# New ranks for a planned instruction order: one planner figure, own ranks for the last job

## The chip, the cores and the metric

The kernel runs on one core of a Trainium2 chip. A core has TensorE (PE) for matrix products, VectorE (DVE), ScalarE (ACT), GpSimd (POOL) and SyncE (SP), which here issues all transfers. Each engine works through its own queue in the order in which the program issued the instructions; they meet at semaphores. The metric is the device time of one execution in microseconds, lower is better. The page of the profile shows one profiled execution.

## The reference

The inputs are q, k and v of 4 batches, 8 heads, 768 positions and 64 elements. Attention keeps the first 4 positions (the sinks) and a window of 128:

```python
keep = is_sink | in_window          # pos < 4, or 0 <= row - column < 128
scores = np.where(keep, scale * q @ k.T, -1e9)
a = softmax(scores); attn = a @ v
```

The result, as 3072 tokens x of 512 elements, goes through a soft mixture of 8 experts with 4 slots each:

```python
logits = x @ phi                               # 3072 x 32
d = softmax over the tokens (logits)
slot_input = d.T @ x                           # 32 x 512
slot_out[e] = np.maximum(slot_input[e] @ w1[e], 0) @ w2[e]
c = softmax over the slots (logits)
out = c @ slot_out                             # 3072 x 512
```

Everything is float32. The expert weights are 32 MB; all of them are loaded once.

## The kernel before, in words

The attention is done in 12 jobs (line 690): for each of 4 batches three blocks of 256 positions with all 8 heads. A job n is made of steps:

- loads of k, q and v from HBM (`load`, line 712), into buffers that the next job uses again;
- `prep` (729): q and k are transposed by TensorE and copied out of PSUM to `qt` and `kt`;
- `softmax` (765), four tiles a job: scores on TensorE (rank S) into one of two `s` tiles of PSUM, masks and maxima on VectorE (M), exponentials on ScalarE (E), then the reciprocal of the sum on VectorE and the product with it on GpSimd (N), then copies of the sinks' weights on GpSimd (K0);
- `weights_transposed` (841, T), `sinks_transposed` (851, K) and `select` (863, sel), by which GpSimd cuts the window out of the transposed weights;
- `values` (875, val): the product with v, copied to `xt`, a single buffer;
- `natural` (906, xn): `xt` transposed to `xn`; and `moe.tokens` (307, tok): the logits of the job's tokens, their running maximum, exponentials, and the products that add up the slots' inputs.

A function `transpose` (699) makes each unit of transpositions: 16 small ones on TensorE for a pair of PSUM tiles, 8 in the first job's halves.

After the last job `moe.finish` (399, fin) closes the sums, and `moe.tail` (511) runs the two expert layers and the combination with c, with an order written out by hand. Before it, `stack` and `turn` (481, 494; tr) prepare c: a split into two parts on GpSimd and a transposition. The weights go through 24 slots of 1 MB; some of these hold attention data until the last jobs have read them.

The order of all steps up to the tail is set by a planner in the program itself (class `Plan`, line 141). Each step is added with a rank (`key`), its engine or a choice of two, and a figure for its time. `order` (167) fills the queues greedily. It keeps a time per engine; of the steps that could start at nearly the same earliest moment it takes the one with the lowest rank:

```python
_, t, i = min((steps[i][0], t, i) for t, i in at if t <= t0 + 0.02)
```

On TensorE the margin is 0.1, and a step with another mode of the array has 2.0 added to its rank and 0.15 (`SWITCH`) to its start. A rank in the table `CFG` (line 624) is an offset: job n uses `4.0 * n + x` (line 935), and tile `tl` of its softmax adds `tl`. The times are used only to make the order; the program has no clock, and on the chip each instruction waits for its operands. Matmuls of rank 900 and over are filler that keeps TensorE's clock up where it has nothing else to do.

Of the kernel before, what the change touches and what calls it, by code (L numbers as in the profile page):

```python
# [19 lines left out]
P = 128  # L20
# [120 lines left out]
class Plan:  # L141
# [19 lines left out]
    def add(self, key, eng, time, fn, r=(), w=(), new=None, last=None, mode=(128, 128)):  # L161

        self.steps.append((key, eng, time if isinstance(time, tuple) else (time,) * len(eng), fn,
                           tuple(r), tuple(w), () if new is None else new if isinstance(new, tuple) else (new,), last))
        self.modes.append(mode)
# [434 lines left out]
class Weights:  # L600
# [8 lines left out]
    def load(self, t):  # L609
# [3 lines left out]
        else:  # L613
# [7 lines left out]
NSLOT = 24  # L621
WARM = 8, 10, 64
PT = 3
CFG = {'prep': [12.61, 9.18],
       'load': [-3.38, -3.85],
       'v': [1.83, 0.85],
       'S': -10.57,
       'M': 2.63,
       'E': -12.68,
       'N': -12.34,  # L630
       'K0': 21.52,
       'T': [-16.0, -7.72],
       'K': -4.71,
       'sel': [-0.03, 28.43, 20.14, 29.01],
       'val': [24.82, -9.08, 25.23, 14.39],
       'xn': [-7.99],
       'tok': [6.92, -6.01, -11.1, -10.96, -2.5, 24.5, -4.05, 10.05, 14.87, -0.52, -10.02],
       'sm': 52.69,
       'sinks': 20.14,
       'tr': [105.63, 140.0, 48.77, 112.98, 90.29, 94.54, 115.57, 123.47, 139.69, 140.0, 40.36, 140.0, 113.15, 139.74, 77.9,  # L640
              132.05, 74.81, 133.34, 53.28, 101.21, 10.99, 140.0, 113.6, 29.98, 113.36, 90.1, 140.0],
       'w': [105.83, 8.0],
       'fin': [67.08, 31.69, -10.5, 14.26, -12.91, 95.11, 15.87, 23.84, 30.35, 16.96],
       'xn1': [13.16],
       'tok1': [-3.74, -12.85, -0.16, -12.31, 11.68, 14.4, -13.13, -12.37, -0.07, -12.63, 13.3]}


def window_path(ctx, tc, c, moe, q, k, v, phi, w1, w2, out):
# [50 lines left out]
    def transpose(key, srcs, r):  # L699

        hs = plan.psum(), plan.psum()

        def go(e):
            for a, src in enumerate(srcs()):
                for x in range(2):
                    i = slice(64 * x, 64 * x + 64)
                    nc.tensor.transpose(hs[x]["tile"][:, 64 * a:64 * a + 64], src[i], c.ident[i, i])

        add(key, "P", 0.45 if len(r) > 1 else 0.25, go, r=r, w=[h["name"] for h in hs], new=hs, mode=ROWS)
        return hs  # L710

    def load(key, n, kind, i):
# [128 lines left out]
    def weights_transposed(key, n, quad):  # L841
        gs = [4 * n + 2 * quad + odd for odd in range(2)]
        hs = transpose(key, lambda: [pts[g % PT][:, a, o:o + P] for g, o in zip(gs, (0, 4)) for a in range(4)],
                       [("pt", g % PT) for g in gs])
        for i in range(2):
            add(key, *COPY, lambda e, h=hs[i], i=i: copy(
                e, xws[quad][:, i, 0].rearrange("p h (o y) -> p o h y", o=2),
                h["tile"].rearrange("p (o h y) -> p o h y", o=2, h=4)),
                r=[hs[i]["name"]], w=[("xw", quad, i, 0)], last=hs[i])
# [83 lines left out]
    for n, (b, j) in enumerate(jobs):  # L933
        def t(x, n=n):
            return 4.0 * n + x

        for kind in range(2):
            for i in range(2):
                load(t(O["load"][kind]), n, kind, i)
            prep(t(O["prep"][kind]), n, kind)  # L940
        for i in range(2):
            load(t(O["v"][i]), n, 2, i)
        for tl in range(4):
            softmax({x: t(tl + O[x]) for x in ("S", "M", "E", "N", "K0")}, n, tl)
            if tl % 2:
                weights_transposed(t(O["T"][tl // 2]), n, tl // 2)
        if j == 0:
            add(t(O["sinks"]), "V", 0.9, lambda e, b=b: batch_sinks(nc, vsink, c, b), r=["v4s", "bm"], w=["vsink"])
        sinks_transposed(t(O["K"]), n)
        for quad in range(2):  # L950
            for i in range(2):
                select(t(O["sel"][2 * quad + i]), n, quad, i)
        for quad in range(2):
            values([t(x) for x in O["val"][2 * quad:2 * quad + 2]], n, quad)
        end = "1" if n == N - 1 else ""
        natural(t(O["xn" + end][0]), n)
        moe.tokens(plan, [t(x) for x in O["tok" + end]], b, j, half, xnb, (0, 1))
        if j == NJ - 1:
            if b == B - 1:
                moe.finish(plan, [t(x) for x in O["fin"]])  # L960

                for _ in range(WARM[2]):
                    h = plan.psum("s")
                    add(900.0, "P", 0.11, lambda e, h=h: nc.tensor.matmul(
                        h["tile"][:, 0, 0:64], lhsT=c.ident, rhs=c.ident[:, 0:64], start=True, stop=True),
                        r=[("sk", 0, 0)], new=h, last=h)
            last = ["sit"] if b == B - 1 else []
            moe.slot_softmax(plan, t(O["sm"]), b, [("lg", b, x, i) for x in range(NJ) for i in range(2)] + last)
# [237 lines left out]
```

## Time and profile before

| | us |
|---|---|
| median of 3 runs | 248.84 (248.19 to 251.78) |
| profiled execution | 248.67 |
| its span, first to last instruction | 247.0 |
| TensorE busy | 214.8 (87% of the span) |
| VectorE, ScalarE, GpSimd busy | 161.3, 151.1, 141.9 |
| HBM read, written | 52.53 MB, 6.29 MB |

Nearly all instructions are issued through a wrapper at line 127, so groups are told apart by the tiles that they write and read: `w` and `s` are PSUM tiles, `first` holds loaded q and k and later `xn` and `xt`, `wt` is any of the 1 MB slots (in the attention `kt`, the softmax's weights and v, later expert weights), `ident` is the identity of the transpositions. A row of a timeline gives the start in us from the span's start, the duration, engine, line, operation, tiles and count. A row of the busy time by stage gives the stage, its length, and for each engine the busy us and the number of instructions, then the clock granted to TensorE as a share of the full one, the share of the DMA engines and the GB/s. A row of waits gives who waited for whom: us in total, times, longest.

### The profile page before, as it was taken

Reading aid. Unit: us, or ns where it says so; the run is one execution under the profiler, and the core shown is the slowest. Engines: PE = TensorE matmul, PEld = TensorE weight load, DVE = VectorE, ACT = ScalarE, POOL = GpSimd, SP = SyncE. Lnnn points to the kernel's source line nnn. Section 1 sums busy time; section 2 is a strip of 40 time slices with the busy share of each in tenths; the row PEclk is TensorE's granted clock in tenths of the full one; section 3 lists DMA queues with packets and bytes.
Section 4 is the critical chain, followed back from the end, with each engine's and each line's share of the span. In section 5 each row is a group of like instructions: output and inputs, shape, how many; then the busy total and the mean of one; then the engine's idle time right before and its main releaser. Section 6 shows DMA issues by size and latency. Waiting matters only on the chain.

```text
span 247.0 us, 8602 instructions
## 1 busy us (share of the span) xinstructions
PE 214.8 (87%) x3356; PEld 152.0 (62%) x3356; DVE 161.3 (65%) x440; ACT 151.1 (61%) x577; POOL 141.9 (57%) x281
## 2 busy tenths in 40 slices
PE   7953899898999799999979899997999999999820
PEld 7733566576777567776747677664787534556520
DVE  4289568759899956889994888997544611225340
ACT  2167569869778886968888686888643411214320
POOL 2036687976857995885789497678995141000000
PEclk9996799999999999999999999999999999999985
DMA  5597989999899799999999999460149989999896
GB/s 117 114 199 157 169 255 280 257 268 287 240 213 285 239 284 262 281 251 205 265 202 245 242 335 198 91 215 1 31 160 330 372 333 344 348 349 367 315 319 204
DMA packets 102963, 59.44 MB, mean 241 GB/s; under 512 B 76292, under 2 KB 98820, under 8 KB 102916
## 3 DMA queue, kind: packets, MB, share of 16 engines
q1 hardware_dynamic: 102916, 58.83, 86.0%
q8 instruction: 28, 0.46, 0.8%
q14 instruction: 19, 0.16, 0.2%
HBM read 52.53 MB, written 6.29 MB: 238 GB/s over the span
## 4 chain that ended last, share of the span: by engine, by line
PE 51%; DVE 28%; ACT 13%; issue 4%; POOL 0%; ACTq 0%; DVEq 0%; POOLq 0%
PE w L127 34%; PE s L127 15%; DVE wt L127 13%; ACT wt L127 9%; DVE s L127 9%; DVE rs L127 2%; PE w L1158 2%; DVE first L127 1%; ACT wt L582 1%; ACT first L127 1%; DVE call L127 1%; DVE acc L127 1%; DVE sums L127 0%; DVE wt L567 0%; DVE vsink L127 0%
## 5 line engine op out<-in xcount | busy, mean ns | idle before, releaser
L127 ACT ACTIVATE wt<-s,wt 128x132 f32<-128x132 f32 x192 | 68.5, 376 | 10.7 <-DVE wt L127 4.5
L127 POOL TENSOR_TENSOR wt<-wt 128x528 f32<-128x528 f32 x96 | 63.8, 670 | 19.4 <-DVE wt L127 8.2
L127 POOL TENSOR_SCALAR_AFFINE_SELECT wt<-wt 128x512 f32<-128x512 f32 x88 | 54.4, 640 | 15.6 <-DVE sums L127 9.8
L127 PE MATMUL w<-wt 128*64 128x128 f32 (+3 forms) x550 | 50.7, 317 | 1.6 <-DVE wt L567 1.0
L127 PE MATMUL s<-wt,qt 64*64 64x196 f32 (+2 forms) x768 | 43.1, 332 | 10.0 <-ACT wt L127 7.0
L127 PEld LDWEIGHTS w<-wt 128*64 128x64 f32 (+2 forms) x550 | 35.9, 140 | 13.8 <-DVE wt L567 2.1
L127 ACT ACTIVATION_READ_ACCUMULATOR wt<-s,wt 128x1 f32 x192 | 40.5, 211 | 0.0
L127 PEld LDWEIGHTS s<-wt,qt 64*64 64x64 f32 x768 | 27.0, 136 | 20.1 <-ACT wt L127 10.5
L127 DVE TENSOR_REDUCE wt<-s 128x4 f32<-128x528 f32 x48 | 33.9, 707 | 1.7
L127 PE MATMUL w<-ident,wt 64*128 64x64 f32 (+1 forms) x442 | 28.9, 239 | 3.7 <-POOL wt L127 1.2
L127 ACT COPY wt<-w 128x512 f32<-128x512 f32 (+1 forms) x41 | 23.7, 581 | 11.7 <-PE w L127 8.6
L127 PEld LDWEIGHTS w<-ident,wt 64*128 64x128 f32 (+1 forms) x442 | 21.2, 142 | 13.2 <-issue 6.6
L127 DVE COPY wt<-w 128x512 f32<-128x512 f32 (+1 forms) x33 | 22.0, 666 | 10.8 <-PE w L127 10.8
L127 PEld LDWEIGHTS w<-ident,first 64*128 64x128 f32 x576 | 21.8, 141 | 10.7 <-issue 5.0
L127 PE MATMUL w<-ident,first 64*128 64x64 f32 x576 | 26.9, 231 | 1.5 <-ACT first L127 1.5
L127 ACT COPY first<-w 128x512 f32<-128x512 f32 x32 | 18.6, 592 | 15.5 <-PE w L127 15.4
L127 DVE COPY_PREDICATED s<-later,s 128x256 f32<-128x256 uint8 x48 | 20.4, 425 | 4.4 <-PE s L127 3.2
L127 DVE TENSOR_TENSOR wt<-wt 128x4 f32<-128x4 f32 x48 | 13.6, 283 | 10.2 <-ACT wt L127 9.0
L127 ACT ACTIVATE qt<-w 128x512 f32<-128x512 f32 (+1 forms) x25 | 14.4, 579 | 6.2 <-PE w L127 4.3
L127 PE MATMUL s<-wt 128*32 128x256 f32 x256 | 14.4, 380 | 0.0
L127 PE MATMUL w<-wt,si 128*32 128x512 f32 x112 | 14.1, 594 | 0.0
L127 POOL COPY wt<-wt 128x512 f32<-128x512 f32 (+2 forms) x13 | 5.7, 455 | 13.5 <-ACT wt L127 11.0
(115 smaller groups left out, 246.1 us busy)
## 6 DMA issues: line engine op xcount, KB each, us to landing
wt<-in_moe_w_dram SPq DMA_DIRECT2D x30, 1024.0 KB, 8.2
wt<-in_v_dram SPq DMA_DIRECT2D x24, 256.0 KB, 4.5
first<-in_q_dram SPq DMA_DIRECT2D x22, 256.0 KB, 5.5
first<-in_k_dram SPq DMA_DIRECT2D x22, 256.0 KB, 4.6
out_dram<-wt SPq DMA_DIRECT2D x4, 1024.0 KB, 7.6
first<-in_moe_w_dram SPq DMA_DIRECT2D x2, 1024.0 KB, 5.1
out_dram<-wt SPq DMA_DIRECT2D x3, 512.0 KB
first<-in_k_dram SPq DMA_DIRECT2D x4, 128.0 KB, 2.3
```

The costliest lines, as they stand in the source:

```text
L127: return self.tc.keep_in_program_order(f(*args, **kw))
L582: (nc.vector.tensor_copy if n % 2 else nc.scalar.copy)(ob[:, 2 * (n - n0):2 * (n - n0) + 2], yp)
L1158: nc.tensor.matmul(t[:, 0:P], lhsT=c.ident, rhs=c.ident, start=True, stop=True)
```

## The change

The planner's figure for a unit of transpositions goes from 0.45 to 0.5 us, for a unit of half the size from 0.25 to 0.27. The last job (n = 11) gets its own ranks for all steps of the softmax, the transposed weights, the selects and the values (`S1` to `val1`); it had its own before for `xn` and `tok` alone. All ranks in `CFG` have new values. No step is added or left out, and nothing else of the planner is changed.

```diff
-CFG = {'prep': [12.61, 9.18],
-       'load': [-3.38, -3.85],
-       'v': [1.83, 0.85],
-       'S': -10.57,
-       'M': 2.63,
-       'E': -12.68,
-       'N': -12.34,
-       'K0': 21.52,
-       'T': [-16.0, -7.72],
-       'K': -4.71,
-       'sel': [-0.03, 28.43, 20.14, 29.01],
-       'val': [24.82, -9.08, 25.23, 14.39],
-       'xn': [-7.99],
-       'tok': [6.92, -6.01, -11.1, -10.96, -2.5, 24.5, -4.05, 10.05, 14.87, -0.52, -10.02],
-       'sm': 52.69,
-       'sinks': 20.14,
-       'tr': [105.63, 140.0, 48.77, 112.98, 90.29, 94.54, 115.57, 123.47, 139.69, 140.0, 40.36, 140.0, 113.15, 139.74, 77.9,
-              132.05, 74.81, 133.34, 53.28, 101.21, 10.99, 140.0, 113.6, 29.98, 113.36, 90.1, 140.0],
-       'w': [105.83, 8.0],
-       'fin': [67.08, 31.69, -10.5, 14.26, -12.91, 95.11, 15.87, 23.84, 30.35, 16.96],
-       'xn1': [13.16],
-       'tok1': [-3.74, -12.85, -0.16, -12.31, 11.68, 14.4, -13.13, -12.37, -0.07, -12.63, 13.3]}
+CFG = {'prep': [14.14, 11.26],
+       'load': [-3.21, -5.66],
+       'v': [-1.5, -2.36],
+       'S': -2.69,
+       'M': -3.97,
+       'E': -13.55,
+       'N': -14.47,
+       'K0': 0.23,
+       'T': [-10.69, -13.82],
+       'K': 3.06,
+       'sel': [28.76, 0.08, 23.88, 3.39],
+       'val': [19.1, 22.33, 30.0, 14.34],
+       'xn': [4.68],
+       'tok': [29.91, 4.21, 24.58, 23.66, 30.0, 23.7, 18.05, 9.45, 30.0, 29.73, 12.4],
+       'sm': 28.75,
+       'sinks': 29.27,
+       'tr': [108.27, 115.31, 110.99, 111.87, 90.92, 75.69, 112.44, 97.39, 124.43, 88.85, 102.8, 105.1, 63.6, 137.13, 99.23,
+              103.23, 57.24, 128.11, 64.92, 73.8, 10.5, 69.95, 110.93, 42.9, 139.73, 94.35, 61.5],
+       'w': [90.76, 8.0],
+       'fin': [-0.34, -7.46, -22.01, 45.38, -18.68, 31.25, 57.82, 91.45, -23.97, -30.0],
+       'xn1': [12.91],
+       'tok1': [0.15, -10.01, 22.09, -11.24, -1.41, -9.06, -16.0, -1.4, -11.95, 1.64, -2.52],
+       'S1': -16.0,
+       'M1': 14.38,
+       'E1': 24.63,
+       'N1': -3.99,
+       'K01': -12.25,
+       'T1': [-12.94, -1.46],
+       'K1': 30.0,
+       'sel1': [9.32, -3.46, 0.09, -14.66],
+       'val1': [19.95, 14.0, -6.45, -11.32]}
...
-        add(key, "P", 0.45 if len(r) > 1 else 0.25, go, r=r, w=[h["name"] for h in hs], new=hs, mode=ROWS)
+        add(key, "P", 0.5 if len(r) > 1 else 0.27, go, r=r, w=[h["name"] for h in hs], new=hs, mode=ROWS)
...
+        end = "1" if n == N - 1 else ""
         for tl in range(4):
-            softmax({x: t(tl + O[x]) for x in ("S", "M", "E", "N", "K0")}, n, tl)
+            softmax({x: t(tl + O[x + end]) for x in ("S", "M", "E", "N", "K0")}, n, tl)
             if tl % 2:
-                weights_transposed(t(O["T"][tl // 2]), n, tl // 2)
+                weights_transposed(t(O["T" + end][tl // 2]), n, tl // 2)
...
-        sinks_transposed(t(O["K"]), n)
+        sinks_transposed(t(O["K" + end]), n)
         for quad in range(2):
             for i in range(2):
-                select(t(O["sel"][2 * quad + i]), n, quad, i)
+                select(t(O["sel" + end][2 * quad + i]), n, quad, i)
         for quad in range(2):
-            values([t(x) for x in O["val"][2 * quad:2 * quad + 2]], n, quad)
-        end = "1" if n == N - 1 else ""
+            values([t(x) for x in O["val" + end][2 * quad:2 * quad + 2]], n, quad)
```

## The prediction

> **What bounds the kernel now.** I read the page first, then the busy time of each engine by stage, then TensorE's waits in the middle of the run, then the timelines of the last job.
>
> ```profile
> span 247.0 us, 8602 instructions
> PE 214.8 (87%) x3356; PEld 152.0 (62%) x3356; DVE 161.3 (65%) x440; ACT 151.1 (61%) x577; POOL 141.9 (57%) x281
> PE 51%; DVE 28%; ACT 13%; issue 4%; POOL 0%; ACTq 0%; DVEq 0%; POOLq 0%
> ```
>
> ```profile
> core 0: us, PE busy (x) PEld busy (x) DVE busy (x) ACT busy (x) POOL busy (x), PEclk, DMA share, GB/s
> 0.00:45.16 45.16, 34.51 (x491) 26.08 (x494) 30.14 (x97) 26.23 (x107) 23.50 (x54) 0.92 0.80 183
> 45.16:87.19 42.03, 39.19 (x701) 28.56 (x701) 35.16 (x94) 33.72 (x136) 32.59 (x62) 1.00 0.95 260
> 87.19:129.34 42.15, 39.30 (x702) 28.70 (x702) 34.95 (x94) 33.94 (x136) 32.58 (x62) 1.00 1.05 249
> 129.34:171.50 42.16, 38.78 (x687) 28.45 (x687) 34.80 (x94) 33.52 (x134) 32.22 (x62) 1.00 0.74 196
> 171.50:195.45 23.95, 23.71 (x328) 18.53 (x327) 11.85 (x32) 12.38 (x43) 17.18 (x38) 1.00 0.57 196
> 195.45:247.00 51.55, 39.28 (x454) 21.71 (x454) 14.37 (x32) 11.33 (x27) 3.84 (x7) 0.93 0.96 325
> ```
>
> TensorE leads the chain of waits with 51%. The stages are cut where the trace repeats: from 45.16 on, one batch (three jobs) takes 42.03, 42.15 and 42.16 us. In each, TensorE is busy for 39.2 us of 42.1, VectorE 35, ScalarE 34, GpSimd 33. So the middle is bound by TensorE but for about 2.8 us a batch. The expert layers and the output begin at 195.45 and take 51.55 us.
>
> Which results TensorE waits for in the middle (45 to 180 us): us in total, times, longest.
>
> ```profile
> PE s L127 <- ACT wt L127: 5.1, 6, 1.2
> PE w L127 <- DVE lb L127: 2.0, 3, 0.9
> PE w L127 <- ACT first L127: 1.5, 3, 0.5
> ```
>
> These are 8.6 us: scores that wait until the exponentials have left a bank of PSUM (5.1), slot products that wait for the evicted weights `lb` (2.0), and transpositions to `xn` that wait for the eviction of the values (1.5). All that an order can win in the middle lies here; the 39 us a batch stay.
>
> **The change, part by part.** No instruction is added or removed; the same 8602 stand in another order on five queues. So every term is a wait that goes or comes.
>
> *The figure.* Sixteen transpositions are one unit:
>
> ```profile
> 88.02 0.71 PE L127 MATMUL w<-ident,first 64*128 64x64 f32 x16
> 88.66 0.50 PE L127 MATMUL w<-pst,vsink 128*128 128x256 f32 x2
> ```
>
> ```profile
> L127 PE MATMUL w<-ident,first 64*128 64x64 f32 x576 | 26.9, 231 | 1.5 <-ACT first L127 1.5
> L127 PE MATMUL w<-ident,wt 64*128 64x64 f32 x384 | 18.3, 231 | 1.9 <-POOL wt L127 1.2 <-ACT qt L127 0.7
> ```
>
> The next work starts 0.64 us after a unit's first (88.66 less 88.02). The planner's old figure with the switch of mode was 0.45 + 0.15 = 0.60, the new one gives 0.65. There are (576 + 384) / 16 = 60 units, so the old plan held TensorE free 60 x 0.05 = 3.0 us too early over the run. This doesn't shorten anything by itself. It also doesn't touch the figures of the copies out of PSUM, 0.51 on ScalarE and 0.61 on VectorE, which run longer:
>
> ```profile
> L127 ACT COPY wt<-w 128x512 f32<-128x512 f32 x39 | 23.0, 592 | 5.5 <-DVE wt L127 2.7 <-PE w L127 2.4
> L127 DVE COPY wt<-w 128x512 f32<-128x512 f32 x31 | 21.1, 682 | 6.8 <-PE w L127 6.8
> ```
>
> So the new plan is right about one engine and still some 0.07 to 0.08 us too early about each copy: not every wait it planned away will be away.
>
> *The middle.* `xn` goes from -7.99 to 4.68, over three jobs of 4 later in rank: the transpositions no longer jump in front as soon as the planner thinks the values are copied, and something else may stand between. I take their 1.5 us as gone. The maxima go from 2.63 to -3.97, so on VectorE they now precede the token maxima (-6.01 to 4.21), the `lb` copy (-4.05 to 18.05) and the sums (-0.52 to 29.73). That could shorten the 5.1 us on the exponentials; but at the first job of a batch VectorE masks as well as reduces, and these waits may be pure latency, so I count nothing. The `lb` copy falls in rank: its 2.0 us I leave as they are. Middle: -1.5 us, bounds -8.6 (all waits gone) and +5.4 (worked out under the slower rival).
>
> *The last job.* Its keys are now its own. In the trace it waits on GpSimd (rows of GpSimd, one of VectorE, then of TensorE):
>
> ```profile
> 176.99 0.29 POOL L127 CAST qt<-call 128x128 fp32r<-128x128 f32 x1
> 177.37 0.47 POOL L127 TENSOR_TENSOR qt<-call,qt 128x128 fp32r<-128x128 f32 x1
> 177.80 0.62 POOL L127 TENSOR_SCALAR_AFFINE_SELECT wt<-wt 128x512 f32<-128x512 f32 x1
> 178.40 1.06 POOL L127 TENSOR_TENSOR wt<-wt 128x528 f32<-128x528 f32 x1
> 179.42 0.62 POOL L127 TENSOR_SCALAR_AFFINE_SELECT wt<-wt 128x512 f32<-128x512 f32 x1
> 180.00 0.20 POOL L127 CAST wt<-wt 128x32 fp32r<-128x32 f32 x1
> ```
>
> ```profile
> 177.55 0.18 DVE L127 RECIPROCAL wt<-wt 128x4 f32<-128x4 f32 x1
> ```
>
> ```profile
> 181.35 1.32 PE L127 MATMUL s<-ident 128*128 128x64 f32 x10
> ...
> 182.54 0.48 PE L127 MATMUL w<-pst,vsink 128*128 128x256 f32 x2
> ```
>
> The last tile's reciprocal ends at 177.73, but its product on GpSimd starts at 178.40: a stack for the output (`qt<-call`) and a select went first, 0.67 us. Its sink copies start at 180.00, behind another select that was put between, 0.58 us. Meanwhile TensorE runs filler (`s<-ident`) from 181.35 until the sinks' weights are there at 182.54. In ranks (4 x 11 for the job, 3 for the tile): that stack had 53.28, the last tile's sink copies 47 + 21.52 = 68.52; now the stack has 64.92 and the copies 47 - 12.25 = 34.75, ahead of three of the four selects (53.32, 40.54, 44.09, 29.34). The product (47 - 3.99 = 43.01) is ahead of the stack too. I count 0.67 + 0.58 = 1.25, cut to 1.2, because the filler gives room for 182.54 - 181.35 = 1.19. Bounds: -4.1 if all filler went (34 matmuls at about 0.12 us, 1.19 / 10, from the rows above and the group below) and +1.5 if the two stacks pushed back (0.76 us each: 177.80 less 176.99, and as much again) end up in front of the expert layers.
>
> ```profile
> L127 PE MATMUL s<-ident 128*128 128x64 f32 x34 | 5.2, 278 | 0.0
> ```
>
> The chain behind the last values, up to 195.45, is serial with filler between; I leave it. The expert layers keep their 51.55 us as long as the weights come:
>
> ```profile
> 181.58 7.28 SPq L127 DMA_DIRECT2D wt<-in_moe_w_dram  x4
> 193.59 0.37 SPq L127 DMA_DIRECT2D first<-in_moe_w_dram  x1
> 197.40 20.81 SPq L127 DMA_DIRECT2D wt<-in_moe_w_dram  x9
> ```
>
> ```profile
> wt<-in_moe_w_dram SPq DMA_DIRECT2D x30, 1024.0 KB, 8.2
> ```
>
> ```profile
> 195.45:225.20 29.75, 29.06 (x322) 15.02 (x325) 9.24 (x24) 7.61 (x20) 3.84 (x7) 1.00 1.04 347
> ```
>
> Fourteen tiles (4 + 1 + 9) of 1024 KB, 1.05 MB, are issued from 181.58 on; at the 347 GB/s of the last row that is some 42 us, to about 224. The second half of that stage's products, behind 225.20, needs the last of them. I estimate that cover at 1 to 3 us. As the tiles' slots are freed by the last jobs, an earlier end moves both; if only the products moved, a gain beyond 3 us would be lost to DMA.
>
> *The start.* The first job's loads of v now come ahead of phi and the sink rows on SP; both are used many us later, and I count nothing. What matters here is TensorE's clock (last columns: clock, DMA, GB/s):
>
> ```profile
> 14.03:20.86 6.83, 3.38 (x60) 2.35 (x62) 5.65 (x22) 5.14 (x26) 3.34 (x6) 1.00 1.15 220
> 20.86:27.69 6.83, 4.78 (x56) 3.36 (x54) 4.61 (x11) 2.94 (x11) 5.46 (x11) 0.50 0.92 176
> 27.69:34.52 6.83, 5.80 (x103) 4.15 (x100) 5.13 (x13) 5.81 (x27) 4.59 (x8) 1.00 0.81 224
> ```
>
> After a stretch in which TensorE was busy for 3.38 of 6.83 us, the next 6.83 us ran at half clock; after one with 4.78 busy it was full again. If the new order fills the first stretch, up to 4.78 / 2 = 2.4 us are won; if another stretch is halved, up to 6.83 / 2 = 3.4 us are lost. I take nothing: few steps are ready then, and ranks decide only between ready ones.
>
> The Trainium skill ("TensorE: Matmul & The Clock Gate", Part 1) has the clock halved after an idle window of about 3.4 us. No gap of that length stands in this stretch, so the trace doesn't agree with that wording: here a busy half was enough. By the page alone, a second half-clock stretch (below, among the rivals) would need such a gap and have next to no chance; by the trace it keeps a small one.
>
> **The sum.** The profiled execution took 248.67 us, of which 247.0 are the span. 248.67 - 1.5 - 1.2 = 246.0; the median shown, 248.84, is 0.17 above the profiled one, so I say 246.1.
>
> **The rivals.**
>
> *Most waits go.* The search finds an order that fills two thirds of the 8.6 us (5.7) beside the last job's 1.2: 248.84 - 6.9 = 241.9. For it: VectorE, ScalarE and GpSimd each have 7 us or more free in a batch, and low-ranked token work can be slipped into TensorE's gaps. Against: the copies' figures are still short, and in the row of waits ScalarE, not TensorE's own length, was late.
>
> *The new figure does nothing on the chip.* The waits change place and sum to the same: 248.8. For it: TensorE had been later than planned, which hides the other engines' lateness; a plan packed tightly to a right figure shows it again.
>
> *Half clock a second time.* 248.84 + up to 3.4, say 251.5. It needs one more 6.83 us stretch near the start with half or less busy; the stretch from 27.69 has 5.80.
>
> *Slower: the token chain is starved.* Logits go from 6.92 to 29.91, behind the first values of the next job (4 + 19.1 = 23.1). The values can't be copied to `xt` until the logits have read the old ones. Where the values' product runs first, its PSUM bank stays held, and logits, `lb` and products then come due with nothing left to put between. Price: one wait as that for `lb`, 2.0 / 3 = 0.67 us, in each of 11 jobs, less the 2.0 that are there: +5.4, so 254.2. It decides from the point where, in most jobs, TensorE goes idle with the logits of the job before unfinished. Against it: the planner knows this dependence.
>
> **How the numbers follow.** Forecast 0.42, most waits go 0.20, nothing 0.22, half clock 0.06, starved tokens 0.10. The range 241.5 to 251.5 leaves out a quarter of the second, a third of the fourth and all of the fifth: 0.05 + 0.02 + 0.10 = 0.17. The forecast alone spans 244 to 248.5. Two per cent of 248.84 is 5.0 us, about what a measurement of this kernel can tell from no change: below 243.9 lie nine tenths of the second case and a tenth of the forecast, 0.18 + 0.04 = 0.22; above 253.8 six tenths of the last, 0.06; between, 0.72.
>
> **What would show it.** Right: the batches take 41.6 us (1.5 us over three), the wait for `first` is gone from TensorE's list, and the expert layers start near 192.7 with the same 51.5 us behind them. The last job's product on GpSimd would start as its reciprocal ends, and less filler would run before its values. Wrong: a batch over 42.1 us, waits of TensorE for `lb` or for evicted values in every job, a second stretch at half clock before 45 us, or expert layers longer than 52 us because weights come late. If the middle is unchanged and the start differs by 2 us or more, the term that I set to nothing was the one that counted.

## The result and the profile after

The changed kernel takes 257.31 us (median; 254.67 to 257.51) where the kernel before, beside it, took 249.18. The ratio is 1.031, with a 95% interval of 1.026 to 1.036: slower. The forecast of 246.1 missed, and so did its range of 241.5 to 251.5. The profiled execution took 257.51 us, 255.7 of them the span.

From the page of the kernel after: the span, the busy times, and TensorE's clock in 40 slices.

```profile
span 255.7 us, 8637 instructions
PE 224.6 (88%) x3362; PEld 156.8 (61%) x3362; DVE 166.9 (65%) x437; ACT 152.3 (60%) x580; POOL 143.0 (56%) x281
PEclk9967599999998999998899999889999999999995
```

TensorE has six records of matmuls more (all filler; a matmul that isn't a transposition leaves two records in these traces) and yet is busy 9.8 us longer (224.6 to 214.8). The clock row says where to look: a dip over three slices at the start (6, 7, 5) and an 8, or two, at three places in the middle. The same row of the kernel before has a dip over two slices at the start and none in the middle:

```profile
PEclk9996799999999999999999999999999999999985
```

The busy times of the kernel after by stage (columns as in the prediction: stretch and length, busy time and count of each engine, clock, DMA share, GB/s). The cuts are laid so that each stage holds TensorE's instructions of before to within ten.

```profile
0.00:46.74 46.74, 36.91 (x483) 28.68 (x485) 32.57 (x97) 26.17 (x107) 23.56 (x54) 0.85 0.75 172
46.74:91.06 44.32, 41.58 (x707) 29.27 (x707) 36.40 (x92) 33.22 (x133) 32.80 (x62) 0.96 0.88 249
91.06:135.38 44.32, 41.56 (x705) 29.55 (x702) 36.56 (x94) 34.41 (x138) 32.83 (x62) 0.96 0.95 249
135.38:179.75 44.37, 40.95 (x689) 28.95 (x685) 36.34 (x94) 34.29 (x137) 32.83 (x62) 0.96 0.71 179
179.75:204.27 24.52, 24.33 (x338) 19.38 (x335) 10.80 (x33) 12.83 (x44) 17.10 (x38) 1.00 0.54 194
204.27:255.70 51.43, 39.27 (x455) 21.00 (x454) 14.23 (x32) 11.34 (x27) 3.85 (x7) 0.94 0.96 324
```

Against the rows of before, the start is 1.6 us longer (46.74 to 45.16), the three batches 2.3, 2.2 and 2.2, the last job 0.6 (24.52 to 23.95), the expert layers 0.1 shorter. These add up to the 8.7 us by which the span grew. In a batch the idle time is the same (44.32 - 41.56 = 2.76 after, 42.15 - 39.30 = 2.85 before); the busy time grew, at a mean clock of 0.96 where 1.00 stood.

The stretches of the kernel after, up to the expert layers, in which the granted clock is 0.50:

```profile
14.30:21.13 6.83, 5.64 (x71) 4.61 (x73) 5.86 (x15) 3.43 (x16) 3.76 (x8) 0.50 0.86 167
24.55:31.37 6.82, 6.10 (x66) 4.42 (x66) 4.29 (x12) 2.41 (x10) 3.36 (x8) 0.50 0.41 67
75.75:79.16 3.41, 3.41 (x22) 1.92 (x16) 1.81 (x5) 2.12 (x13) 2.22 (x5) 0.50 1.00 405
120.12:123.53 3.41, 3.41 (x22) 1.94 (x16) 1.79 (x5) 2.06 (x12) 2.17 (x5) 0.50 0.88 242
164.49:167.91 3.42, 3.42 (x22) 1.94 (x16) 1.77 (x5) 2.04 (x12) 2.15 (x6) 0.50 0.02 5
sum 23.89, PE 21.97 PEld 14.82 DVE 15.52 ACT 12.06 POOL 13.66; mean PE 4.39 PEld 2.96 DVE 3.10 ACT 2.41 POOL 2.73
```

TensorE works 21.97 us at half clock; before it was the 4.78 us of the one stretch that the prediction shows. At full clock that work takes half the time, so the growth costs (21.97 - 4.78) / 2 = 8.6 us. That is the size of the whole loss, in the two profiled executions.

A second account of the same, over one stretch from 8 us to the start of the expert layers (before, then after):

```profile
8.00:195.45 187.45, 169.03 (x2871) 123.97 (x2871) 144.42 (x387) 138.31 (x548) 136.80 (x263) 0.98 0.85 222
```

```profile
8.00:204.27 196.27, 178.88 (x2878) 129.38 (x2878) 150.18 (x384) 139.44 (x551) 137.86 (x263) 0.94 0.80 212
```

Idle is the length less the busy time: 18.4 before, 17.4 after, so the new order has 1.0 us *less* idle time. Taking half of the half-clock work off the busy time leaves 166.6 and 167.9 us of work: 1.3 more, of which some 0.7 is the six records of filler (0.12 us each). The rest of the difference is the clock. Both accounts rest on one profiled execution of each kernel.

**Why the clock fell in the middle.** TensorE in the windows of equal length that end where the three half-clock stretches begin:

```profile
72.33:75.75 3.42, 1.86 (x23) 1.18 (x26) 3.29 (x11) 3.28 (x13) 3.34 (x8) 1.00 1.06 259
116.70:120.12 3.42, 1.85 (x24) 1.18 (x26) 3.26 (x12) 3.33 (x13) 3.34 (x7) 1.00 1.06 211
161.08:164.49 3.41, 1.84 (x27) 1.18 (x26) 3.25 (x11) 3.36 (x13) 3.33 (x7) 1.00 0.37 84
```

It is busy for 54% in each. The stretches at half clock begin whole multiples of 3.41 us apart: from 75.75 to 120.12, and from there to 164.49, it is 44.37 us, 13 times 3.413. So the clock is set in windows that lie on one grid through the trace. The least busy window on the grid of the kernel before, in its middle, had 2.18 of 3.41 us, 64%, and the clock stayed at 1.00 behind it:

```profile
164.22:167.63 3.41, 2.18 (x60) 1.53 (x56) 3.34 (x10) 3.18 (x19) 2.72 (x6) 1.00 0.48 131
```

Laid at any place, not only on the grid, the least busy 3.41 us of the three batches of before hold 2.30, 2.31 and 2.05 us of work (from 82.68, 124.82 and 166.40). So the idle time of a batch hasn't grown; the new order has gathered it at one place, the third job. There is one thing more. A batch with its stretch takes 44.32 to 44.37 us, 13 windows, so the gap falls on the same place of a window in each batch, while the 42.15 us of a batch of before are 12.35 windows. That the stretches repeat for this reason is worked out from the lengths, not tested. TensorE's timeline in the third job of the first batch, with the idle time before a group and what ended it in brackets, and the waits of the whole middle (46 to 180 us):

```profile
72.93 0.71 PE L127 MATMUL w<-ident,wt 64*128 64x64 f32 x15 [0.49 <-ACT lt L127]
73.87 0.33 PE L127 MATMUL w<-ident,lt 128*128 128x128 f32 x1 [0.23 <-ACT qt L127]
74.34 0.52 PE L127 MATMUL w<-ident,wt 128*128 128x128 f32 x2
75.56 0.96 PE L127 MATMUL w<-first,lb 128*32 128x256 f32 x8 [0.69 <-DVE call L127]
```

```profile
PE s L127 <- ACT wt L127: 3.6, 9, 1.2
PE w L127 <- DVE call L127: 2.1, 3, 0.7
PE w L127 <- ACT lt L127: 1.5, 3, 0.5
PE w L127 <- DVE pst L127: 1.0, 1, 1.0
PE w L127 <- ACT qt L127: 0.7, 3, 0.2
```

The waits for `lb` (2.0) and nearly all of those for `first` (1.5) are gone, as are 1.5 us of those for the exponentials; the waits for `call`, `lt`, `pst` and `qt` came. The sum was 8.6 us and is 8.9.

What made `lt` late stands on VectorE, ScalarE and GpSimd (rows of each, in that order; the step `sums<-sums` is the minimum that merges the new token maximum, which is kept negated, with the old one):

```profile
70.64 0.80 DVE L127 TENSOR_TENSOR vsink<-wt,bm 128x512 fp32r<-128x512 f32 x1
71.37 1.02 DVE L127 TENSOR_TENSOR sums<-sums 128x1 f32<-128x1 f32 x1
...
75.19 0.22 DVE L127 COPY call<-w 128x64 f32<-128x64 f32 x1
```

```profile
72.42 0.36 ACT L127 ACTIVATE lt<-w,sums 64x128 f32<-64x128 f32 x1 [1.00 <-DVE sums L127]
```

```profile
70.87 1.50 POOL L127 TENSOR_TENSOR wt<-wt 128x528 f32<-128x528 f32 x1
```

A minimum of 128 single values took 1.02 us; one of the same steps in the kernel before takes 0.16 (at 110.99). It began beside a large product on GpSimd and ended (72.39) as that ended (72.37). The exponentials of the token weights on ScalarE needed that minimum and waited 1.00 us for it, and TensorE waited 0.49 us for them. Behind the minimum VectorE then works off four steps of the maxima (72.59 to 74.7) before it copies `call`, and the PSUM bank that the slot products need is held until that copy is done. The copy's rank (the last of `tok`) went from -10.02 to 12.4 and that of the maxima (`M`) from 2.63 to -3.97, so the two changed places.

### The profile page after: what moved, and what is told of

It is laid out like the page before. It is cut to its first block, busy times and chain, and to the rows that moved or that the text cites. A ratio compares the mean times of both kernels' runs of the same rounds, so it can differ in the third digit from the quotient of the medians.

```text
span 255.7 us, 8637 instructions
## 1 busy us (share of the span) xinstructions
PE 224.6 (88%) x3362; PEld 156.8 (61%) x3362; DVE 166.9 (65%) x437; ACT 152.3 (60%) x580; POOL 143.0 (56%) x281
## 4 chain that ended last, share of the span: by engine, by line
PE 55%; DVE 22%; ACT 16%; issue 3%; POOL 0%; ACTq 0%; DVEq 0%; POOLq 0%
PE w L127 40%; PE s L127 14%; ACT wt L127 12%; DVE wt L127 9%; DVE s L127 6%; DVE sums L127 3%; DVE first L127 2%; PE w L1167 1%; ACT wt L582 1%; ACT first L127 1%; ACT lt L127 1%; DVE vsink L127 1%; ACT sums L127 0%; DVE wt L567 0%; DVE phi L127 0%
## 5 line engine op out<-in xcount | busy, mean ns | idle before, releaser
L127 POOL TENSOR_TENSOR wt<-wt 128x528 f32<-128x528 f32 (+1 forms) x96 | 64.4, 674 | 29.3 <-DVE wt L127 22.1
L127 PE MATMUL w<-wt 128*64 128x128 f32 (+3 forms) x550 | 53.6, 330 | 1.9 <-DVE wt L567 1.0
L127 PE MATMUL s<-wt,qt 64*64 64x196 f32 (+2 forms) x768 | 45.0, 340 | 10.2 <-ACT wt L127 3.9
L127 PEld LDWEIGHTS w<-wt 128*64 128x64 f32 (+2 forms) x550 | 37.7, 147 | 15.5 <-issue 2.5
L127 ACT ACTIVATION_READ_ACCUMULATOR wt<-s,wt 128x1 f32 x192 | 41.9, 218 | 0.0
L127 ACT COPY wt<-w 128x512 f32<-128x512 f32 (+1 forms) x45 | 25.5, 581 | 13.6 <-PE w L127 10.9
L127 PE MATMUL w<-ident,wt 64*128 64x64 f32 (+1 forms) x442 | 30.5, 245 | 2.3 <-ACT lt L127 1.5
L127 DVE COPY wt<-w 128x512 f32<-128x512 f32 (+1 forms) x29 | 18.9, 655 | 11.4 <-ACT wt L127 7.6
L127 DVE COPY first<-w 128x512 f32<-128x512 f32 x25 | 17.0, 679 | 8.0 <-PE w L127 7.8
L127 ACT COPY first<-w 128x512 f32<-128x512 f32 x23 | 13.7, 594 | 8.6 <-PE w L127 8.0
```

Of the source, the lines that this page charges most:

```text
L127: return self.tc.keep_in_program_order(f(*args, **kw))
```

## The experiments

**The two parts apart.** First the figure alone, with the ranks of before:

```diff
-CFG = {'prep': [14.14, 11.26], ...
+CFG = {'prep': [12.61, 9.18], ...     (all ranks of before, for the last job too)
```

> The old ranks with the new figure (0.5 and 0.27) alone. Theory: the new order loses its time by where the new ranks put VectorE's and GpSimd's work at the third job of each batch, and TensorE then runs one stretch of 3.4 us a batch at half clock; the figure alone doesn't do that: 246 to 251 us, no half-clock stretch between 35 and 195 us. Rival: any order made with the new figure leaves TensorE idle more often: 253 us or more.

Measured: 254.65 us (252.94 to 260.31), 1.022 [1.015, 1.029]. The figure alone, on the ranks that stood beside the old one, costs 1.5 to 2.9%. My theory, a figure that does no harm, fell, and the profiled execution (260.31 us) has three stretches at half clock in the middle (from 47.77, 78.50 and 109.22) where I had expected none. But two of the four runs had a mean clock of 0.966, about that of the kernel before beside them (0.965 to 0.967 in four of its eight runs), and still took 252.94 and 253.28 us. So what these two runs lose, 4 to 5 us, can hardly be half clock. No profiled execution shows what it is.

Then the ranks alone, with the old figure:

```diff
-        add(key, "P", 0.5 if len(r) > 1 else 0.27, go, ...
+        add(key, "P", 0.45 if len(r) > 1 else 0.25, go, ...
```

> The new ranks with the old figure (0.45 and 0.25). Theory: the ranks carry the loss: 253 to 258 us. Rival: the ranks are sound and only fit a plan with their own figure; with the other figure the order is reshuffled and the time is anywhere, then the collision of the third job isn't a matter of ranks: 247 to 251 us would speak for that.

Measured: 258.84 us (255.69 to 260.48), 1.033 [1.027, 1.038]. Its interval overlaps that of the change as a whole. Each part loses alone, and together they lose about what the ranks lose. The new ranks are no better with the new figure than with the old one, as far as these runs can tell.

**The last job's own ranks.**

```diff
-            softmax({x: t(tl + O[x + end]) for x in ("S", "M", "E", "N", "K0")}, n, tl)
+            softmax({x: t(tl + O[x]) for x in ("S", "M", "E", "N", "K0")}, n, tl)
                 (the same for "T", "K", "sel" and "val")
```

> The new kernel, but the last job takes the ranks that all other jobs have (softmax, transposed weights, selects, values). My prediction had the last job's own ranks worth 1.2 us: then 258.5 us. Rival: the stretch from the last job's values to the expert layers is as long with either: 257.3 within 0.5 us. If the own ranks do harm: below 256.5 us.

Measured: 259.65 us (259.2 to 260.08), 1.045 [1.044, 1.047]. The own ranks are worth some 2 us, but not where I had put them: from the sink product of the last job to the expert layers this kernel takes 24.40 us, the change 24.52. By the account from 8 us on it has 21.5 us of idle time against 17.4: TensorE's waits for `call` are 3.6 instead of 2.1 us over the three batches, and one wait near 21 us for VectorE is 2.3 us instead of 0.5. How ranks of the last job come to change the order ahead of it was not followed further.

**The minimum out of GpSimd's way.** Here the token maximum stays in PSUM, in a free column of the logits' tile, so that the minimum reads one operand from PSUM and one from SBUF. The order is that of the change to the last step.

```diff
+        first = (lambda: L["tile"][:, P:P + 1]) if n else (lambda: new)
 ...
-            new, L["tile"][:, 0:P], op=ALU.max, axis=AX.X, negate=True), ...
+            first(), L["tile"][:, 0:P], op=ALU.max, axis=AX.X, negate=True), ...
 ...
-            plan.add(key, "V", 0.07, lambda e: nc.vector.tensor_tensor(new, new, old, op=ALU.min),
+            plan.add(key, "V", 0.07, lambda e: nc.vector.tensor_tensor(new, first(), old, op=ALU.min),
```

> The new kernel in its exact order; the token maximum is left in PSUM, so that the step that merges it with the old one (VectorE, 128x1) reads one operand from SBUF instead of two. Theory: in the new kernel this step takes 1.02 us beside a product of GpSimd at the third job of each batch, against 0.15 elsewhere, because the two engines exclude each other there; the exponential, lb and TensorE's products come late by that, and the idle time brings half clock. Then the step falls to about 0.2 us, the three half-clock stretches of the middle (75.7, 120.1, 164.5) go, a batch takes about 42 instead of 44.3 us, and the time is 250 to 252.5 us. Rival: the order alone (maxima ahead of lb) leaves TensorE idle: the step is shorter, the half-clock stretches stay, 256 to 257.5 us.

Measured: 255.01 us (254.58 to 257.07), 1.029 [1.023, 1.034]; the interval overlaps that of the change (1.026 to 1.036), so a gain isn't shown, and the time lies between the theory's range and the rival's. VectorE's timeline at the place that was shown above:

```profile
69.64 0.80 DVE L127 TENSOR_TENSOR vsink<-wt,bm 128x512 fp32r<-128x512 f32 x1
70.45 0.16 DVE L127 TENSOR_TENSOR sums<-w,sums 128x1 f32<-128x1 f32 x1
70.53 0.85 DVE L127 TENSOR_TENSOR wt<-wt 128x4 f32<-128x4 f32 x1
```

The minimum takes 0.16 instead of 1.02 us, and now the next small step with two operands in SBUF takes 0.85: the collision moved on by one step. The mean of all 11 minima says the same (before, after, this kernel; busy us, mean ns):

```profile
L127 DVE TENSOR_TENSOR sums<-sums 128x1 f32<-128x1 f32 x11 | 2.2, 201 | 0.2
```

```profile
L127 DVE TENSOR_TENSOR sums<-sums 128x1 f32<-128x1 f32 x11 | 5.9, 535 | 0.3
```

```profile
L127 DVE TENSOR_TENSOR sums<-w,sums 128x1 f32<-128x1 f32 x11 | 1.7, 158 | 0.6 <-ACT lt L127 0.3
```

So the price of that step comes from GpSimd's work beside it, and hangs on where its operands lie. The Trainium skill ("SBUF — State Buffer", section "Who interferes with whom") has a VectorE instruction with two SBUF inputs contend with a GpSimd instruction that reads SBUF; the trace agrees: 1.02 us with both in SBUF, 0.16 with one of them in PSUM, in the same order.

Of the three half-clock stretches of the middle the one near 75 us is gone; those near 118.0 and 162.4 stayed. That isn't the collision's doing. First the least busy 3.41 us at any place in the first and the second batch, then the windows on the grid that hold most of them:

```profile
71.07:74.48 3.41, 1.79 (x23) 1.02 (x20) 3.28 (x10) 3.36 (x14) 3.33 (x7) 1.00 0.91 229
113.71:117.12 3.41, 1.79 (x23) 1.02 (x20) 3.28 (x10) 3.36 (x14) 3.33 (x7) 1.00 1.13 225
```

```profile
70.23:73.64 3.41, 2.32 (x35) 1.50 (x35) 3.29 (x8) 3.14 (x13) 3.33 (x6) 1.00 0.72 163
114.60:118.02 3.42, 1.88 (x13) 0.90 (x13) 3.29 (x9) 3.42 (x18) 3.25 (x8) 1.00 1.05 205
```

The gap is the same in both batches, and as wide as in the change (1.79 us of work, there 1.84 to 1.86). But the grid, counted back from the stretch at 118.02 by 14 windows to 70.23, cut it otherwise in the first batch: the window held 2.32 us, and the clock stayed at 1.00. So this run doesn't show that the collision gathers the idle time. It shows something better: what one stretch costs in the same kernel and the same execution. From the third job of one batch to the third job of the next, without a stretch and with one:

```profile
75.06:117.69 42.63, 39.79 (x705) 28.61 (x701) 36.23 (x93) 34.34 (x138) 32.63 (x62) 1.00 0.95 249
117.69:162.06 44.37, 41.75 (x706) 29.51 (x702) 36.15 (x94) 34.04 (x136) 32.72 (x62) 0.96 0.90 240
```

The same work takes 1.74 us longer, about half of the 3.41 us at half clock; the idle time is 2.84 and 2.62 us. And a batch of the new order at full clock is still 0.5 us longer than one of before (42.63 against 42.15 us), with the same idle time (2.85) and TensorE busy for 39.79 instead of 39.30 us.

**Filler in the gap.** Small products on the identity, in the third job of each batch only: two ahead of the transposition of `lt`, six ahead of the slot products.

```diff
+            if n % 3 == 2:
+                for _ in range(6):
+                    nc.tensor.matmul(S["tile"][:, 0:64], lhsT=c.ident, rhs=c.ident[:, 0:64], start=True, stop=True)
                 (ahead of the slot products; two such into T["tile"] ahead of the transposition of lt)
```

> The new kernel in its exact order, with filler added on TensorE at the third job of each batch only: 2 small products (128x64) into the empty PSUM tile before the transposition of lt and 6 into the empty tile before the slot products, where TensorE stood idle 0.2 and 0.7 us. Nobody waits for them. Theory (half clock is what costs): TensorE is busy for about 80% instead of 54% of the stretch before, the three half-clock stretches of the middle go, each worth half of 3.41 us = 1.7: 257.3 - 5.1 = 252.2 us, range 251 to 253.5. Rival (the half clock only falls into time in which TensorE has slack, the other engines set the pace): the stretches go, but the time stays within 1.5 us of 257.3; or they stay, because filler of that kind doesn't count: 257 to 259.

Measured: 258.08 us (257.31 to 266.23), 1.033 [1.024, 1.041], no gain, as the rival had it. The same with the minimum in PSUM as well:

> The filler of the run before this one and the token maximum left in PSUM, together. Theory: the collision of VectorE and GpSimd and the half clock are two costs: the collision is worth some 0.7 us by itself (2.4 us measured, less one half-clock stretch of 1.7 that went with it), so about 251.5 us. Rival: it acted only by way of the half clock: as with the filler alone, within 0.5 us.

Measured: 264.82 us (260.63 to 266.69); the runs spread too far for an interval, and neither expectation came true. TensorE at the place, in the kernel with both:

```profile
74.71 1.52 PE L127 MATMUL w<-ident 128*128 128x64 f32 x12 [0.63 <-DVE call L127]
```

The filler writes to the tile of the slot products, so it waited for the same bank that they wait for. It stood behind the gap, not in it, and added 1.5 us a batch. So neither run is the test that it was meant to be. Two readings are still of use. With the filler alone four of five runs had a mean clock of 0.964 or 0.965, where the change had 0.938 to 0.948, and yet took 257.3 to 258.2 us: the clock rose, by some 5.6 us over the span, and the time did not fall. The filler, at 1.5 us in each of four jobs, would eat about that, but no profiled execution shows one of these runs. In the second of the two kernels the window ahead of a half-clock stretch that begins at 118.52:

```profile
115.10:118.52 3.42, 2.31 (x35) 1.46 (x27) 3.29 (x9) 3.37 (x14) 3.34 (x7) 1.00 1.05 234
```

Here 2.31 of 3.42 us busy, 68%, was followed by half clock, where 64% in the kernel before was not. The busy share alone doesn't decide. In this window stood, behind the end of a unit of scores, transpositions and products with 64 columns. The Trainium skill ("TensorE: Matmul & The Clock Gate", Part 4) says that transpositions don't count as busy in the same way; that fits this window, but no run here tried transpositions against products at the same share.

**A dense product in the gap.** Placed where nothing holds it up: behind the transpositions of the sinks of the jobs 3, 6 and 9, into the free half of their own PSUM tile, one product of 128x128 by 128x256 with a weight tile, which is loaded anyway, as its data.

```diff
+            if n and n % 3 == 0:
+                nc.tensor.matmul(h["tile"][:, 256:512], lhsT=c.ident, rhs=wts[0][:, 0:256], start=True, stop=True)
```

> The new kernel in its exact order, with one dense product (128x128 by 128x256, a loaded weight tile as data) added behind the sinks' transpositions of jobs 3, 6 and 9, in the empty half of their PSUM tile. That place is the idle 0.7 us ahead of the slot products; the tile is free there, which the tile of the filler before was not. Theory: half clock is the loss. TensorE's work at half clock falls from 21.8 us by the 3 x 3.4 us of the middle, half of which is time: 257.3 - 5.1 = 252.2, range 251 to 254. If only some stretches go, 1.7 us for each that goes. Rival (half clock only fills time that TensorE would wait anyway): the stretches go and the time stays above 256.

Measured: 254.43 us (253.0 to 257.1), 1.019 [1.015, 1.024], against 1.031 [1.026, 1.036] for the change; just above the theory's range. TensorE at the place in the second batch, and the two windows of the grid on which the gap falls there:

```profile
120.49 0.60 PE L127 MATMUL w<-wt,ident 128*128 128x256 f32 x2
121.36 0.64 PE L127 MATMUL w<-first,lb 128*32 128x256 f32 x8 [0.27 <-DVE call L127]
```

```profile
116.24:119.65 3.41, 2.58 (x52) 1.80 (x48) 3.34 (x9) 2.36 (x12) 3.41 (x4) 1.00 0.78 173
119.65:123.07 3.42, 3.00 (x25) 1.69 (x27) 3.29 (x9) 3.42 (x17) 2.75 (x8) 1.00 1.03 226
```

In the second and third batch the wait for `call` shrank to 0.27 and 0.26, and the clock stayed at 1.00. The least busy 3.41 us at any place of the second batch now hold 2.28 us (117.94 to 121.35), where the change has 1.85 in a window. So the product narrows the gap, but here the grid cuts it in two as well, and the run doesn't part the two causes. The first batch kept its stretch, near 75 us, 6.83 us long in the profiled execution (256.15 us): TensorE still waited 0.76 us for `call`, and the window ahead held 2.33 of 3.41 us, 68%. A batch without a stretch takes 42.78 and 43.01 us where the change takes 44.32 and 44.38 between the same two products. So with more work in it such a batch is faster by some 1.4 to 1.5 us. With the 1.74 us of the run with the minimum in PSUM, that makes the clock the cause of most of a batch's growth of 2.2 us, whatever set it.

**The kernel before, with longer warm-up.** The other side of the same question: does half clock cost the kernel before anything that filler can win back?

```diff
-WARM = 8, 10, 64
+WARM = 8, 40, 64
```

> The kernel before with up to 40 instead of 10 pieces of filler that the planner may put on TensorE where it has nothing else, which is at the start. Theory: the half-clock stretch from 20.9 to 27.7 us goes, worth up to 2.4 us there: 246.4 to 248 us. Rival: the start is bound by the other engines' latencies, or filler delays the work behind it by 0.2 us each: 248.5 to 250 us.

Measured: 249.83 us (248.19 to 251.2), 1.001 [0.997, 1.005]. The stretch moved to 30.85 and halved, to 3.4 us, but TensorE spent 13.3 us on this filler where 3.7 stood, and the last products with the sinks' weights of the start came 1.8 us later (48.37 against 46.55). The rival, which said that filler delays the work behind it, was right.

**The kernel before, with two small changes to VectorE's work.** The minimum's operand in PSUM as above, and the addition of 1e-9 to the sums left out.

```diff
+        first = (lambda: L["tile"][:, P:P + 1]) if n else (lambda: new)     (and its two uses, as above)
-            nc.vector.tensor_tensor(z, z, eps, op=ALU.add)
```

> The kernel before in its exact order, with the token maximum left in PSUM and without the addition of 1e-9 to the softmax's sums (which are at least 1 there), so that VectorE has two kinds of small steps less that read two operands from SBUF. If collisions cost the kernel before too: VectorE loses some 10 us of busy time (48 steps of 283 ns, 11 of 201), of which a tenth to a fifth may lie on the path: 246.5 to 248 us. Rival: they lie beside TensorE's work: 248.2 to 249.2 us.

Measured: 246.32 us (244.1 to 247.68), 0.989 [0.980, 0.997]: the fastest kernel here. One of its batches:

```profile
86.74:127.74 41.00, 39.35 (x705) 28.62 (x701) 32.18 (x83) 34.15 (x136) 32.72 (x62) 1.00 1.05 254
```

VectorE has some eleven steps less in a batch (94 to 83), and TensorE's idle time falls from 2.85 to 1.65 us in a batch with the busy time where it was (39.30 to 39.35). In this kernel VectorE's small steps do set part of the idle time, 1.2 us a batch. The two edits were not run apart.

**The change with these two, and with the dense product too.** First the two on the changed kernel:

> The new kernel in its exact order with both small changes that gained 1.1% on the kernel before: the token maximum left in PSUM, and no addition of 1e-9 to the softmax's sums (which are at least 1). Theory (idle time adds to half clock, and both go down together): VectorE has fewer steps that can collide with GpSimd, idle falls by some 3 to 5 us, one or two half-clock stretches go: 249 to 253 us. Rival: with the maxima ranked ahead, VectorE's collisions are off TensorE's path but for the one already removed: 254.5 to 255.5 us, as with the maximum alone.

Measured: 248.59 us (246.54 to 250.1), 0.997 [0.993, 1.002] of the kernel before: the theory's way, and 0.4 us below its range.

Then these and the product behind the sinks' transpositions:

> All three together: both small changes and the dense product. Theory: the middle runs without half clock; what stays of the loss is the start's second stretch (up to 3.4 us): 247 to 250.5 us. Rival: the new order is slower than the old one also at full clock: with the same small changes the old order took 246.3, so more than 251 us without half clock in the middle.

Measured: 248.81 us (246.73 to 250.96), 0.996 [0.991, 1.001]. In its trace no batch has a stretch at half clock, and the wait for `call` is 0.5 us in all instead of 2.1. The time is that of the kernel before, without touching the order of the change; but the product adds nothing here to what the two edits give alone, and the order of before, with the same two edits, takes 246.32 us. So of a loss of 8 us some 2.5 are left when like is compared with like. Half a microsecond a batch of that is what the new order costs at full clock: with the two edits alone a batch takes 41.50 us (73.25 to 114.75), and 41.00 in the order of before. No run shows the rest.

The account from 8 us to the expert layers, for the profiled execution of each kernel (us; the work is the busy time with half of the half-clock work taken off). The two kernels with one part of the change alone and the first with filler are left out, because their profiled execution was well above their other runs.

| kernel | idle | TensorE's work at half clock | work as at full clock |
|---|---|---|---|
| before | 18.4 | 4.8 | 166.6 |
| before, longer warm-up | 12.6 | 3.4 | 175.0 |
| before, two small changes | 13.2 | 8.9 | 165.3 |
| after | 17.4 | 22.0 | 167.9 |
| after, last job on common ranks | 21.5 | 18.4 | 167.6 |
| after, minimum in PSUM | 18.5 | 15.1 | 167.5 |
| after, filler and minimum | 17.8 | 22.0 | 173.6 |
| after, dense product | 17.2 | 17.5 | 168.8 |
| after, two small changes | 15.1 | 12.4 | 167.9 |
| after, both and dense product | 13.4 | 6.7 | 169.2 |

The third column is the one that sets the change apart from the kernel before. The last two rows lose it step by step (22.0, 12.4, 6.7), and 4.0 us of idle time with it.

## Why the prediction was wrong, step by step

**What bounds the kernel.** "All that an order can win in the middle lies here; the 39 us a batch stay." The second half is the step that failed. I had treated TensorE's busy time as given and only its waits as open to the order. The busy time of a batch went from 39.30 to 41.56 us. Of these 2.26 us, the half clock explains 3.41 / 2 = 1.71. The other 0.55 is there at full clock too (39.79 us in the batch without a stretch of the kernel with the minimum in PSUM); what makes it stays open. I had read the clock row and named the clock for the start alone, where a stretch at half clock already stood.

**The figure.** "This doesn't shorten anything by itself" was right but too mild: alone it costs 2.2% [1.5, 2.9]. It moves steps that had been ranked for the other figure; which of them cost the time was not followed.

**The middle, -1.5 us.** The named wait did go (for `first`, 1.5 to 0.2). But the rival "the waits change place and sum to the same" describes the waits: 8.6 us before, 8.9 after. I had judged the maxima's fall in rank harmless, and had not named the copy of `call`, whose rank rose past theirs. Four steps of the maxima now stand ahead of it, and TensorE waits 0.69 us for it in each batch. The measured middle is +6.7 us (three batches), outside of the term's bounds of -8.6 and +5.4, because the bounds held waits only.

**The last job, -1.2 us.** It came out at +0.2 (24.32 to 24.52 from the same product to the expert layers; by the stage rows, which cut it by the count of instructions, +0.6), with 40 records of filler instead of 34. GpSimd in the last job after:

```profile
186.96 1.07 POOL L127 TENSOR_TENSOR wt<-wt 128x528 f32<-128x528 f32 x1
187.97 0.30 POOL L127 CAST qt<-call 128x128 fp32r<-128x128 f32 x1
188.34 0.46 POOL L127 TENSOR_TENSOR qt<-call,qt 128x128 fp32r<-128x128 f32 x1
188.75 0.21 POOL L127 CAST wt<-wt 128x32 fp32r<-128x32 f32 x1
```

A select that starts at 186.35 and takes 0.64 us still holds the product up, for 0.33 us behind the reciprocal. Between the product and the sink copies no select stands any more, but a stack (187.97) still goes ahead of the sink copies (188.75), though its rank of 64.92 is far behind their 34.75. From the reciprocal's end to the sink copies it took 2.27 us before (180.00 - 177.73) and takes 2.12 now (188.75 - 186.63): 0.15 won of the 1.25 that I had counted. I had taken ranks for an order. The planner takes the step that can start first, and lets the rank decide only among steps whose starts lie within 0.02 us (line 225); a step that follows another on the same engine counts as ready 0.05 us after it (line 243). So a stack that is ready at that moment beats the copies at any rank. This is argued from the code and borne out by the rows; no run tried another margin.

**The start, 0.** Measured +1.6 us, so the term that I set to nothing counted. The second half-clock stretch came, 24.55 to 31.37, with 6.10 us of work in it, 3.05 us lost, and the first held 5.64 us of work instead of 4.78. Against this stand 0.8 us less idle time (10.65 before, 9.83 after, from the stage rows) and some 1.1 us less work in the stage. I had read the clock over 6.83 us, 3.38 of them busy. On the grid that is one window with 1.90 us of work, behind which the clock stayed at 1.00, and one with 1.48, behind which it fell. "Half clock a second time" named the mechanism and the place, at 251.5 us and a chance of 0.06; what it lacked were the three stretches in the middle, 3 x 1.7 us. So it had the right mechanism, at one of four places.

**The expert layers, unchanged at 51.5 us.** Right: 51.43. The weights came in time.

**Slower, the token chain starved, 254.2.** The sign was right, the mechanism in part: a PSUM bank that is held too long does make TensorE idle, at 0.69 us a time where 0.67 was the price. It does so in three jobs instead of eleven, and about repays the 2.0 us of the wait for `lb`. The slow side was reached by another way.

**The page's rule on the clock.** The prediction set the idle window of the Trainium skill ("TensorE: Matmul & The Clock Gate", Part 1) against a trace in which a busy half was enough, and kept a small chance. The trace decides again: behind 54% busy, with no single gap above 0.69 us in the rows of that window, the clock fell in all three batches. Nor did a gap of nearly that length always do it. In the kernel with the last job on common ranks TensorE stood still for 3.39 us from 11.49 on; two windows shared that, with 1.62 and 1.82 of 3.41 us busy, and the clock stayed at 1.00. In the change the same wait (from 11.98 on) left 1.09 us in one window, and half clock followed. That the stretches here come in lengths of 3.41 and 6.83 us agrees with the window that the page gives.

## What to carry to other kernels

Busy time on the bounding engine is not a constant of the work: before an order is called free, look for the window, as long as the shortest dip in the clock row, in which it leaves that engine least busy, and treat a new low as a cost of its own. Idle time spread thin can be cheaper than the same idle time in one place. When a dip vanishes in an experiment, look whether the gap went or only the window's place in it. And where a planner schedules greedily, a rank is an order only among steps that it holds for ready together; read its margin before working out what a rank will do.

## What the runs showed of the hardware

TensorE's clock falls to half for one or more windows of 3.41 us, on one grid through a trace, behind a window in which TensorE did little; a long gap isn't needed. The busy share alone doesn't tell which window that is. In the change 54% led to half clock three times. In the kernel before 64% in the middle didn't, nor did 56% at the start. At 68% it went both ways: half clock in the kernels with the dense product (2.33 of 3.41 us) and with filler and minimum (2.31), full clock with the minimum alone (2.32). Where the line lies, and what counts, stays open. Where the grid falls decides as well: of two gaps with 1.79 us of work in 3.41, one was followed by half clock and the other not. One stretch of 3.41 us made a batch 1.74 us longer.

A VectorE step on 128 single values can take 1.02 us instead of 0.16 when a large GpSimd product runs beside it and both of its operands are in SBUF. That product took 1.50 us where the next one took 1.06, but not for the minimum's sake: in the kernel with the minimum in PSUM it took 1.50 us as well (at 69.86). In both it began beside a VectorE product of 0.80 us that also reads two tiles (`vsink<-wt,bm`), which is the likely cause.

The same kernel varies, and its clock with it: the change with the two small edits ran from 246.54 us, at a mean clock of 0.980, to 250.1 us, at 0.949.
